# Attention and mixture of experts on one core: the cost table and the ranks of an instruction planner are replaced

## The chip, the core and the metric

The kernel runs on one core of a Trainium2 chip. TensorE (PE in the profile), VectorE (DVE), ScalarE (ACT), GpSimd (POOL) and SyncE (SP) each take their instructions in the order of the program; between engines semaphores keep the order. DMA transfers are issued from SP (loads and stores of the attention part) and from POOL (expert weights, gathers and scatters by index). The metric is the device time of one execution in microseconds (us), lower is better; it is given as the median of several runs.

## The reference

```python
scores = scale * np.matmul(q, k.transpose(0, 1, 3, 2))          # 2 batches, 8 heads, 576 tokens, 64
x = (np.log1p(np.abs(rel)) / psi_i)[..., None]                  # rel: distance of two positions
bias = np.maximum(x @ w1 + b1, 0.0) @ w2                        # 1 -> 32 -> 8 heads, for each pair
attn = softmax(scores + bias)
x = np.matmul(attn, v), heads joined                            # 1152 tokens of 512
logits = x @ w_gate                                             # 8 experts
expert_idx, gate_w = argmax(logits), softmax(logits) at it
# an expert takes at most capacity = 288 tokens, in the order of the tokens
out[token] = gate_w * (relu(x @ w1[e]) @ w2[e])                 # 512 -> 1024 -> 512; 0 if not taken
```

## The kernel before, in words

**Attention.** The work is cut into 40 units: two batches, five row tiles of 128 tokens (the last of 64), four head pairs. A unit n has scores on TensorE (`S`, L195 or L203), a minimum with the bias added on VectorE (`L`, L212), the exponential on ScalarE (`X`, L219), transposes on TensorE (`R` and `T`, L227 to L266), their copies out of PSUM (`C`, L250 and L273) and the product with V (`V`, L289 to L295).

**Bias.** The bias depends on the two positions alone. It is computed once in 36 blocks: hidden rows on three engines (`H`, L122 to L126), a matmul (`M`, L141), an eviction (`E`, L154 or L156) and a store to a scratch tensor in DRAM (`D`, L162, tensor `bd`). Row tiles of it are read back with a skew (`B`, L175 or L178, tile `bt`) as soon as the stores that they need are done. The first scores that can be finished are those of the short row tile t = 4, whose bias comes from the first four blocks.

**Experts.** When a row tile is done, its gate logits are made (`BL`, `BT`, `BC`) and its rows are turned, scaled and stored to DRAM (`BM`, `BX`, `BD`, tensor `xd`). After groups of row tiles the tokens are counted for each expert (`GA`, `GB`, `GK`; the count in PSUM is compared at L451 to L457) and the experts with most tokens are chosen (`P`). For the chosen expert z = 0, 1 (and z = 2 for one small block of tokens) the places of its tokens are matched (`MT`, `FE`), copied to a tile `slots` (`FC`, L475, on ScalarE or VectorE), turned by a small matmul (`FT`, L480), made into indices (`FD`, L486 to L489) and used to gather the rows from `xd` (`FG`, L493, POOL, tile `xe`). The expert's weights come in eight pieces of 512 KB (`WL`, L686, POOL, tile `raw`), which are split into a high and a low part (`WH`, L668 or L670; `WO`, L673, tile `wl`), since each product is made of three matmuls. `XM` turns the gathered rows, `FM` is the first layer (L723, twelve matmuls), `FH` and `FL` split its result (`hh`, `hl`, L726 and L730), `Y` the second layer (L764, groups of six matmuls), `YC` and `OT` turn it back, `OY` scales it (L742 or L744), `OS` scatters it to the output (L748, POOL). z = 2 has steps of its own: `xs`, `xsh`, `xsl` (L803 to L809), `SQ`, `ST`, `SH`, `SL`, `Z` (L828). `RC` (L580) and `RL` then count what is left, for experts beyond these three.

**What sets the order.** All of this is written as 1,126 tasks: `task(name, engines, us, fn, after, rank, takes, late, kb)`. `place_tasks` plays them against a clock: of the tasks whose predecessors are placed and whose buffers come free, those that could begin within 0.3 us of the earliest are compared by rank, and the lowest is issued on its engine. The order found so is the order of the program on each engine; the times are used for nothing else. A rank is a number in the code plus an entry of the table `shift` by kind of task. A DMA task has `kb`: the planner keeps one time `moved` for all transfers and lets each land when the one before it has landed, or a fixed time after its issue, plus its `kb` at 390 per us. `late` is a further time until the result counts as there.

The engines start with the same instructions in both kernels (the constants and the first loads); what follows the planned part (experts beyond the first three) is behind a branch.

Of the kernel before, what the change touches and what calls it, by code (L numbers as in the profile page):

```python
# [18 lines left out]
B, H, S, D = 2, 8, 576, 64  # L19
# [9 lines left out]
def kernel(ctx: ExitStack, tc: tile.TileContext, cap, ins, out):  # L29
# [858 lines left out]
    def rest_begin():  # L888
# [3 lines left out]
        for k in range(8):  # L892
# [9 lines left out]
    tasks = {}  # L902


    shift = {('C', True): 4.5, ('E', False): 1.5, ('E', True): 1.5, ('FL', 0): -0.5, ('FM', 0): 4, ('GA', 0): 0.5,
# [8 lines left out]

    def kind(name):
        if not isinstance(name, tuple):
# [29 lines left out]
    def then(*name):  # L946

        return ("then", name)

    TURN = 0.5  # L950

    def place_tasks(start):
        free_at = dict(start)
        array = None
        ends, begun, held, left, moved = {}, {}, {}, dict(tasks), 0.0
        while left:
            best = []
            for name, (engines, us, fn, after, rank, takes, late, kb) in left.items():
                if any((a[1] if a[0] == "then" else a) not in ends for a in after):
                    continue  # L960
                own = engines if len(engines) == 1 and engines != "s" else None
                ready = max([begun[a[1]] if a[0] == "then" else ends[a] if begun[a, "on"] != own else begun[a] for a in after], default=0.0)
                chosen = []
                for pools, users in takes:

                    at = []
                    for pool in pools:
                        seen = held.get(pool, [])
                        k = len(seen) + chosen.count(pool) - bufs[pool]
                        if k < 0:  # L970
                            at.append((0.0, pool))
                        elif k < len(seen) and all(u in ends for u in seen[k]):
                            at.append((max(ends[u] for u in seen[k]), pool))
                    if not at:
                        break
                    t, pool = at[0] if at[0][0] <= ready else min(at)
                    ready = max(ready, t)
                    chosen.append(pool)
                if len(chosen) == len(takes):
                    e = min(engines, key=lambda e: (max(free_at[e], ready) + us[e], e))  # L980
                    turn = e == "e" and array not in (None, shape(name)[0])
                    best.append((max(free_at[e], ready), rank + TURN * turn, name, e, chosen))
            first = min(b[0] for b in best)
            at, rank, name, e, chosen = min((b for b in best if b[0] <= first + 0.3), key=lambda b: (b[1], b[0]))
            engines, us, fn, after, rank, takes, late, kb = left.pop(name)
            for pool, (pools, users) in zip(chosen, takes):
                held.setdefault(pool, []).append(users)
            took = us[e]
            if e == "e":
                took += 0.096 * (array not in (None, shape(name)[0]))  # L990
                array = shape(name)[1]
            free_at[e] = at + took
            ends[name] = at + took + after_us[e] + late
            begun[name], begun[name, "on"] = at + took, None if late else e
            if kb:
                moved = max(moved, at + took + 0.7) + kb / 390.0
                ends[name] = moved
            fn(*([e] if len(engines) > 1 else []), *(p for p, (pools, _) in zip(chosen, takes) if len(pools) > 1))

    def chain(name, engines, us, gen, after=(), rank=0.0, takes=()):  # L1000
# [10 lines left out]
    for n, blk in enumerate(blocks):  # L1011
        m = span(blk)
        rank = -8.0 + n if n < 4 else 4 * ((n - 4) // 8) - 1.0 + 0.4 * ((n - 4) % 8)
        for c in range(4):
            engines = "p" if c == 3 and n >= 4 else "dap" if c == 2 and n >= 4 or c == 3 else "da"
            task(("H", n, c), engines, {"d": 0.12 + m * 1.1e-3, "a": 0.2 + m * 0.83e-3, "p": m * 3.4e-3},
                 (lambda e="p", n=n, c=c: hidden(n, c, e)), 
                 after=[("H", n - 3, k) for k in range(4)] if n >= 3 else [], rank=rank - 1.2, takes=[("hid", [("M", n)])])
        task(("M", n), "e", 0.06 + m * 1.67e-3 + 0.06 * (m > 512), (lambda w=None, n=n: bias_mm(n, w or bias_psum(n)[0])), after=[("H", n, c) for c in range(4)], rank=rank,
             takes=[(bias_psum(n), [("E", n)])])  # L1020
        task(("E", n), "da", {"d": 1.0, "a": 0.98}, (lambda e, n=n: bias_out(n, e)), after=[("M", n)], rank=rank + 0.1,
             takes=[("bo", [("D", n)])])
        task(("D", n), "s", 0.45, (lambda n=n: bias_store(n)), after=[("E", n)], rank=rank, kb=340)

    for i, (b, t) in enumerate(order):
        n0 = unit0[b, t]
        if i:
            task(("Q", b, t), "s", 0.45, (lambda b=b, t=t: dma_q(b, t)), after=[slot(n0 - 8), then("B", 0, 4, 1)], rank=n0 - 5.0,
                 takes=[("q", [("S", n0 + 3)])], kb=256)
        if (b, t) == (1, 0):  # L1030
            continue
        for g in range(4 if t < 4 else 2):
            users = [("L", n0 + g, z) for z in range(2)] if t < 4 else [("L", n0 + 2 * g + z, 0) for z in range(2)]
            if (b, t) == (0, 0):
# [1 line left out]
            k = order.index((0, t))  # L1036
            dep = [("D", n) for n in (range(4) if t == 4 else range(8 * k - 4, 8 * k + 4))]
            task(("B", b, t, g), "s", 0.45 if t < 4 else 1.2, (lambda b=b, t=t, g=g: dma_bias(b, t, g)), after=dep + [slot(n0 - 6)],
                 rank=n0 - 2.0 + g, takes=[("bt", users)], kb=690)
    for hp in range(4):  # L1040
        task(("K", 1, hp), "s", 0.45, (lambda hp=hp: dma_k(1, hp)), after=[slot(8 + 2 * hp)], rank=17.0, kb=288)
        for b in range(2):
            users = [("V", unit0[b, t] + hp) for t in range(NT)]
            task(("VL", b, hp), "s", 0.45, (lambda b=b, hp=hp: dma_v(b, hp)), after=[slot(17) if b else slot(hp - 1) or then("B", 0, 4, 1)],
                 rank=20.0 * b + hp - 1, takes=[("v", users)], kb=320)
    task("wg", "s", 0.45, lambda: nc.sync.dma_start(out=wgt, in_=ins["wg"]), after=[slot(1)], rank=4.0, kb=32)
    task("route", "s", 2.7, route_const, after=[slot(6)], rank=12.0, kb=300)

# [28 lines left out]
    for i, (b, t) in enumerate(order):  # L1077
# [7 lines left out]
        task(("BC", b, t), "d", 0.8, (lambda b=b, t=t: tile_c(b, t)), after=[("BT", b, t)], rank=n + 1.3)  # L1085
        task(("BM", b, t), "e", 0.48, (lambda w="pt", b=b, t=t: tile_b(b, t, w)), after=[("BL", b, t)], rank=n + 1.2, takes=[(spare, [("BX", b, t)])])
        task(("BX", b, t), "d", 0.64, (lambda b=b, t=t: tile_x(b, t)), after=[("BM", b, t), ("BC", b, t)], rank=n + 1.5, takes=[("x", [("BD", b, t)])])
        task(("BD", b, t), "s", 0.45, (lambda b=b, t=t: tile_d(b, t)), after=[("BX", b, t)] + ([then("FG", 1, 2), then("FG", 2, 0)] if i > 7 else []), rank=n + 1.3, kb=256)
    for g in range(3):
        n = (22.0, 34.0, 44.0)[g]  # L1090
        chain(("GA", g), "d", [0.5, 0.7, 0.3], group_a(g), after=[("BC", b, t) for b, t in groups[g]] + ["route"]
# [17 lines left out]
    for z in range(3):  # L1109
# [7 lines left out]
        for a in range(na):  # L1117
            task(("FG", z, a), "p", 1.25, (lambda z=z, nt=nt, a=a: fetch_rows(z, X[z // 2], nt, a)),
                 after=[("FD", z), ("pools", "clear", "late")[z]] + [("BD", *bt) for g in range(2 if z else 1) for bt in groups[g]],
                 rank=r, late=4.2 if z < 2 else 3.0)  # L1120
    task("pools", "p", 1.4, ffn_pools, after=[("D", n) for n in range(36)] + [slot(18)], rank=20.0)
    task("late", "p", 0.6, late_pools, after=[("V", n) for n in range(NU - 4, NU)] + ["pools"], rank=40.0)
    for a in range(3):
        task(("O", a), "s", 0.45, (lambda a=a: fill_out(a)), after=["pools", slot(33 + a)], rank=34.0, kb=768)
    task("clear", "p", 1.4, lambda: nc.gpsimd.memset(X[0], 0.0), after=[("XM", 0, k) for k in range(4)], rank=33.0)

    for z in range(3):
        for c in range(8):
# [5 lines left out]
            else:  # L1134
# [3 lines left out]
                wait = [] if z == 1 else [("Y", 0, 3, 3)] if c < NW else [("FM", 1, 2 * (c - NW) + 1)]  # L1138
            raw = (lambda c=c, nraw=nraw: RAW[c % nraw])
            task(("WL", z, c), "p", 1.0, (lambda z=z, c=c: weights_load(z, c)), after=dep + [("P", z), then("WL", z, c - 1) if c else then("WL", z - 1, 7) if z else None],  # L1140
                 rank=r, takes=takes, kb=524)
            task(("WH", z, c), "ad", {"a": 0.97, "d": 0.66}, (lambda e, z=z, c=c, raw=raw: split_hi(e, wbuf(z, c)[0], raw())),
                 after=[("WL", z, c)] + wait + (["late"] if z == 1 else []), rank=r + 2)
            task(("WO", z, c), "d", 1.14,
# [205 lines left out]
```

## Time and profile before

| | us |
|---|---|
| median of 3 runs | 278.26 |
| lowest, highest | 274.85, 279.24 |
| the profiled execution's own time | 276.28 |
| its span, first to last instruction | 274.6 |
| TensorE busy | 243.3 (89% of the span) |
| VectorE, ScalarE, GpSimd busy | 194.6, 180.2, 107.3 |
| mean granted TensorE clock | 0.974 of full |

The profile is of one execution, whose own time lies 1.7 us above its span. A share of the whole span hides stages: the stretches and the single waits have to be read one by one. "Granted clock" is the share of TensorE's 2.4 GHz that it was given; 0.5 is 1.2 GHz.

### The profile page before, as it was taken

Reading aid. Unit: us, or ns where it says so; the run is one execution under the profiler, and the core shown is the slowest. Engines: PE = TensorE matmul, PEld = TensorE weight load, DVE = VectorE, ACT = ScalarE, POOL = GpSimd, SP = SyncE. Lnnn points to the kernel's source line nnn. Section 1 sums busy time; section 2 is a strip of 40 time slices with the busy share of each in tenths; the row PEclk is TensorE's granted clock in tenths of the full one; section 3 lists DMA queues with packets and bytes.
Section 4 is the critical chain, followed back from the end, with each engine's and each line's share of the span. In section 5 each row is a group of like instructions: output and inputs, shape, how many; then the busy total and the mean of one; then the engine's idle time right before and its main releaser. Section 6 shows DMA issues by size and latency. Waiting matters only on the chain.

```text
span 274.6 us, 7405 instructions
## 1 busy us (share of the span) xinstructions
PE 243.3 (89%) x2820; PEld 188.2 (69%) x2820; DVE 194.6 (71%) x544; ACT 180.2 (66%) x412; POOL 107.3 (39%) x112
## 2 busy tenths in 40 slices
PE   1995989989999999999969999989989699989950
PEld 0631546557655788888757788878879699979930
DVE  3984989979578666588867975858857779786100
ACT  4897798979899876778857987745232366241400
POOL 2999899999570200000115130120055154500130
PEclk9999999999999999999997999999999979999995
DMA  6589999799698751797698999030145981820030
GB/s 161 206 272 288 373 299 361 230 337 349 188 361 325 250 193 42 219 355 236 175 357 240 347 290 371 17 117 2 41 135 189 375 335 41 264 92 2 2 98 7
DMA packets 26619, 58.63 MB, mean 213 GB/s; under 512 B 3572, under 2 KB 4340, under 8 KB 26576
## 3 DMA queue, kind: packets, MB, share of 16 engines
q1 hardware_dynamic: 22224, 43.02, 47.1%
q0 software_dynamic: 4352, 15.06, 16.4%
q8 instruction: 24, 0.39, 0.6%
q14 instruction: 19, 0.16, 0.2%
HBM read 41.36 MB, written 16.99 MB: 212 GB/s over the span
## 4 chain that ended last, share of the span: by engine, by line
PE 43%; issue 10%; DMA 8%; DVE 6%; POOL 4%; ACT 3%; POOLq 1%; DVEq 0%; ACTq 0%
PE s L195 10%; PE av L289 9%; DMA raw<-in_w_dram 5%; PE tt L227 4%; PE pt L723 3%; DMA xe<-xd,sli 3%; PE s L764 2%; POOL out_dram L748 2%; PE tt L141 2%; PE pt L344 2%; PE tt L764 1%; DVE ed L212 1%; ACT wh L668 1%; PE s L203 1%; PE pt L141 1%
## 5 line engine op out<-in xcount | busy, mean ns | idle before, releaser
L122 POOL TENSOR_SCALAR hid<-c_u,nbv 128x400 f32<-128x400 f32 (+17 forms) x48 | 68.7, 1446 | 6.3 <-PE tt L141 4.2
L212 DVE CUSTOM_DVE_ANT_0 ed<-s,bt 128x576 f32<-128x576 f32 x72 | 51.9, 755 | 22.9 <-PE s L227 10.8
L219 ACT ACTIVATE ed<-ed,mn 128x576 f32<-128x576 f32 x72 | 56.0, 785 | 5.8 <-DVE mn L212 5.7
L250 ACT COPY at<-tt 128x512 f32<-128x512 f32 x71 | 39.0, 590 | 17.7 <-PE tt L227 16.1
L195 PE MATMUL s<-kraw,q 64*128 64x288 f32 x256 | 42.2, 436 | 1.8 <-DVE rt L273 1.6
L289 PE MATMUL av<-at,vt 128*64 128x128 f32 x512 | 35.0, 278 | 0.0
L686 POOL DMA_DIRECT2D raw<-in_w_dram x24 | 13.4, 562 | 49.8 <-DVE wl L673 32.3
L195 PEld LDWEIGHTS s<-kraw,q 64*128 64x128 f32 x256 | 24.8, 190 | 11.7 <-issue 4.4
L289 PEld LDWEIGHTS av<-at,vt 128*64 128x64 f32 x512 | 27.5, 136 | 5.3 <-issue 3.8
L124 ACT ACTIVATE hid<-c_u,c_v 128x528 f32<-128x528 f32 (+17 forms) x44 | 28.2, 680 | 2.9 <-DVE c_v L528 2.9
L126 DVE TENSOR_SCALAR hid<-c_u,c_v 128x432 f32<-128x432 f32 (+17 forms) x52 | 29.6, 617 | 0.1
L673 DVE TENSOR_TENSOR wl<-raw,wh 128x1024 fp32r<-128x1024 f32 x24 | 28.6, 1218 | 0.0
L227 PE MATMUL tt<-c_ident,ed 64*128 64x64 f32 x512 | 22.8, 226 | 0.1
L227 PEld LDWEIGHTS tt<-c_ident,ed 64*128 64x128 f32 x512 | 20.0, 141 | 2.9 <-issue 0.4
L668 ACT CAST wh<-raw 128x1024 fp32r<-128x1024 f32 x13 | 13.6, 1046 | 11.3 <-DMA raw<-in_w_dram 8.0
L434 POOL TENSOR_SCALAR tokv<-s 128x5 bf16<-128x5 f32 (+2 forms) x3 | 0.6, 206 | 51.7 <-DVE s L428 51.7
L141 PE MATMUL pt<-hid,c_w2bd 128*32 128x336 f32 (+12 forms) x152 | 18.0, 511 | 2.7 <-ACT bo L156 1.5
L748 POOL DMA_INDIRECT out_dram<-y,sli x7 | 8.5, 1211 | 27.6 <-ACT sh L842 19.3
L141 PE MATMUL tt<-hid,c_w2bd 128*32 128x512 f32 (+11 forms) x152 | 15.6, 474 | 0.2 <-ACT at L250 0.2
L670 DVE CAST wh<-raw 128x1024 fp32r<-128x1024 f32 x11 | 7.6, 695 | 10.5 <-DMA raw<-in_w_dram 9.3
L219 ACT ACTIVATION_READ_ACCUMULATOR ed<-ed,mn 128x1 f32 x72 | 14.7, 204 | 0.0
L156 ACT ACTIVATE bo<-pt,corr,c_rv 128x192 f32<-128x192 f32 (+23 forms) x24 | 13.0, 596 | 2.1 <-PE pt L141 1.9
(266 smaller groups left out, 518.0 us busy)
## 6 DMA issues: line engine op xcount, KB each, us to landing
bt<-bd SPq DMA_DIRECT2D x28, 576.0 KB, 6.1
raw<-in_w_dram POOLq DMA_DIRECT2D x24, 512.0 KB, 5.8
bd<-bo SPq DMA_DIRECT2D x36, 295.5 KB, 5.3
vt<-in_v_dram SPq DMA_DIRECT2D x8, 320.0 KB, 5.5
kraw<-in_k_dram SPq DMA_DIRECT2D x8, 288.0 KB, 4.7
bt<-bd SPq DMA_DIRECT2D x8, 288.0 KB, 7.3
out_dram<-y SPq DMA_DIRECT2D x3, 768.0 KB, 10.8
q<-in_q_dram SPq DMA_DIRECT2D x8, 256.0 KB, 6.4
```

The lines of the kernel that those rows point to most:

```text
L122: nc.gpsimd.tensor_scalar(hid[:, :m], wu[:, :m], nbv[:, w:w + 1], None, op0=ALU.max)
L124: nc.scalar.activation(hid[:, :m], wu[:, :m], AF.Relu, bias=bvw[:, w:w + 1])
L126: nc.vector.tensor_scalar(hid[:, :m], wu[:, :m], bvw[:, w:w + 1], 0.0, op0=ALU.add, op1=ALU.max)
L141: nc.tensor.matmul(ps[32 * c:32 * c + 32, lo:hi], lhsT=w2bd, rhs=hids[n, c][:, lo:hi], start=True, stop=True, tile_position=(0, 32 * c))
L195: nc.tensor.matmul(ps[i][:, r, :HALF], lhsT=q[p, hp], rhs=k[p, r * HALF:(r + 1) * HALF], start=True, stop=True, tile_position=(64 * i, 0))
L212: nc.vector.tensor_tensor_reduce(out=ed.rearrange("p (r j) -> p r j", r=2), in0=ps[:, :, :HALF], in1=bias.rearrange("p (r j) -> p r j", r= ...
L219: nc.scalar.activation(ed, ed, AF.Exp, scale=-1.0, bias=mns.pop((n, i)), accum_out=total)
L227: nc.tensor.transpose(out[r][:w], ed[p, o:o + w], ident[p, p], tile_position=(64 * r, 0))
L250: nc.scalar.copy(o, v)
L289: nc.tensor.matmul(av[p, hp], lhsT=vt[:, j, i], rhs=at[:, 4 * i + j] if j < 4 else rt, start=(j == 0), stop=(j == 4), tile_position=(0, r))
L668: nc.scalar.copy(hi, raw)
L673: (nc.vector if eng == "d" else nc.gpsimd).tensor_tensor(lo, raw, hi.bitcast(F32), op=ALU.subtract)
```

## The change

Two tables of numbers and four rules of the planner are replaced; no task is added, removed or changed in what it computes. (1) `shift`, the corrections to the ranks, is a new table. (2) A transfer lands `kb`/390 after the later of its issue plus 1.2 us (0.7 before) and the landing before it, and its users are then placed 0.9 us (0 before) plus `late` behind that; the `kb` of nearly all transfers are new. (3) Gathers (`FG`) now have a `kb` and stand in the same row of transfers; before they had a fixed 4.2 or 3.0 us. (4) A successor that may run on one of several engines waits for a `late` result too; a comparison of names let it off before. (5) TensorE's tasks count double before 9.0 us.

```diff
-    shift = {('C', True): 4.5, ('E', False): 1.5, ('E', True): 1.5, ('FL', 0): -0.5, ('FM', 0): 4, ('GA', 0): 0.5,
...
+    shift = {('C', True): 1, ('E', False): -1, ('E', True): 5.5, ('FE', 1): 2, ('FE', 2): 1, ('FH', 0): -2,
...
     TURN = 0.5
+    COLD = 9.0
...
             if e == "e":
+                took *= 2 if at < COLD else 1
                 took += 0.096 * (array not in (None, shape(name)[0]))
...
-            begun[name], begun[name, "on"] = at + took, None if late else e
+            begun[name], begun[name, "on"] = at + took, "late" if late else e
             if kb:
-                moved = max(moved, at + took + 0.7) + kb / 390.0
-                ends[name] = moved
+                moved = max(moved, at + took + 1.2) + kb / 390.0
+                ends[name] = moved + 0.9 + late
...
-        task(("D", n), "s", 0.45, (lambda n=n: bias_store(n)), after=[("E", n)], rank=rank, kb=340)
+        task(("D", n), "s", 0.45, (lambda n=n: bias_store(n)), after=[("E", n)], rank=rank, kb=363)
...
-                 rank=n0 - 2.0 + g, takes=[("bt", users)], kb=690)
+                 rank=n0 - 2.0 + g, takes=[("bt", users)], kb=718)
...
-                 rank=r, late=4.2 if z < 2 else 3.0)
+                 rank=r, kb=470 if z < 2 else 160)
...
-                 rank=r, takes=takes, kb=524)
+                 rank=r, takes=takes, kb=568, late=0.8)
```

**What it does to the order, first place: SP at the start.** SP's queue from the stores of the first four bias blocks (tensor `bd_68`) to the first load of that bias (`bt`, two halves of 288 KB a load). Before:

```order
L162 DMA bd_68<-bo 128x591 x4
L105 DMA vt<-in_v_dram 128x640
L162 DMA bd_67<-bo 128x591 x2
L1046 DMA wgt<-in_wg_dram 128x128
L105 DMA vt<-in_v_dram 128x640
L178 DMA bt<-bd_68 64x2x576 x2
L162 DMA bd_67<-bo 128x591 x2
L178 DMA bt<-bd_68 64x2x576 x2
```

Now:

```order
L162 DMA bd_68<-bo 128x591 x4
L162 DMA bd_67<-bo 128x591 x2
L105 DMA vt<-in_v_dram 128x640
L178 DMA bt<-bd_68 64x2x576 x4
L105 DMA vt<-in_v_dram 128x640
L100 DMA q<-in_q_dram 128x512
L162 DMA bd_67<-bo 128x591 x2
```

The gate weights and one V load (64 and 320 KB) moved behind the bias load, and its second pair of halves no longer waits for two stores. On TensorE one more bias block (`M` of n = 11) now stands ahead of the third scores.

**Second place: ScalarE at two copies of `slots`.** ScalarE where the first expert's slots are copied (L475, the row with 288 columns). Before:

```order
L250 COPY at<-tt 128x2x4x64 x2
L219 ACTIVATE ed,sums<-ed,mn 128x576 x2
L668 CAST wh_1734<-raw_1741 128x1024
L475 CAST slots<-pt 128x288
L250 COPY at<-tt 128x2x4x64 x2
```

Now:

```order
L250 COPY at<-tt 128x2x4x64 x2
L219 ACTIVATE ed,sums<-ed,mn 128x576 x2
L250 COPY at<-tt 128x2x4x64
L475 CAST slots<-pt 128x288
L250 COPY at<-tt 128x2x4x64
```

The split of a weight piece (`wh` from `raw`) that stood ahead of the copy is gone from ScalarE; it stands on VectorE, behind the index step that the copy leads to. The third expert's slots (96 columns), on ScalarE, before:

```order
L668 CAST wh_3350<-raw_1742 128x1024
L767 COPY yt<-pt 128x288
L668 CAST wh_3354<-raw_3365 128x1024
L475 CAST slots<-pt 128x96
L668 CAST wh_3358<-raw_3367 128x1024
```

Now:

```order
L332 COPY lT<-s 128x128
L726 ACTIVATE hh<-pt 128x288
L475 CAST slots<-pt 128x288
L726 ACTIVATE hh<-pt 128x288 x2
L475 CAST slots<-pt 128x96
L315 COPY xT<-av 128x4x64
```

The second expert's slots (288 columns) were copied by VectorE before. Both copies now stand among results of the first layer, and all splits of the second expert's weights on ScalarE come later.

**Third place: the last count on VectorE.** VectorE where the third group of tokens is counted (L451, the first of ten small operations up to L457, on which `RC` on TensorE waits). Before:

```order
L673 TENSOR_TENSOR wl_3349<-raw_1741,wh_3348 128x1024
L673 TENSOR_TENSOR wl_3351<-raw_1742,wh_3350 128x1024
L670 CAST wh_3356<-raw_3366 128x1024
...
L673 TENSOR_TENSOR wl_3353<-raw_3364,wh_3352 128x1024
L451 TENSOR_TENSOR m<-pt,rows 128x8
```

Now:

```order
L673 TENSOR_TENSOR wl_1741<-raw_3464,wh_1740 128x1024
L673 TENSOR_TENSOR wl_3447<-raw_3465,wh_3446 128x1024
L673 TENSOR_TENSOR wl_3449<-raw_3466,wh_3448 128x1024
L809 TENSOR_TENSOR xl<-av,xh 128x4x96
L673 TENSOR_TENSOR wl_3451<-raw_3467,wh_3450 128x1024
L673 TENSOR_TENSOR wl_3453<-raw_3468,wh_3452 128x1024
L451 TENSOR_TENSOR m<-pt,rows 128x8
```

Before, the count stood behind the fourth of the second expert's eight pieces, and twelve `wl` steps came after it; now it stands behind the last piece of the third expert. On TensorE `RC` moved with it, from behind the second of the second expert's eight `FM` to behind `SQ` of q = 0.

## Rows read from the trace of the kernel before

**Rows 1.** Windows: a stretch, its length, each engine's busy time (instructions), granted clock, DMA share, GB/s

```profile
20.00:30.00 10.00, 6.79 (x42) 2.31 (x39) 6.20 (x14) 6.68 (x15) 10.00 (x10) 1.00 1.01 316
...
140.00:150.00 10.00, 7.73 (x96) 6.09 (x94) 6.74 (x18) 5.53 (x13) 3.45 (x4) 0.83 0.93 313
...
210.00:220.00 10.00, 7.76 (x67) 7.28 (x65) 6.66 (x14) 4.38 (x10) 3.82 (x8) 0.97 0.97 364
220.00:230.00 10.00, 10.00 (x72) 9.77 (x72) 7.85 (x37) 7.48 (x12) 4.20 (x8) 0.86 0.57 218
...
260.00:270.00 10.00, 4.92 (x22) 3.13 (x20) 0.00 (x0) 0.83 (x2) 3.09 (x4) 0.86 0.26 73
270.00:274.60 4.60, 0.00 (x0) 0.00 (x0) 0.00 (x0) 0.00 (x0) 0.00 (x0) 0.50 0.00 0
sum 274.60, PE 243.26 PEld 188.17 DVE 194.60 ACT 180.17 POOL 107.27; mean PE 8.69 PEld 6.72 DVE 6.95 ACT 6.43 POOL 3.83
```

**Rows 2.** TensorE's waits: what waited for what: us in total, times, longest

```profile
PE pt L480 <- ACT slots L475: 4.5, 2, 2.3
PE s L203 <- DVE mn L212: 3.1, 1, 3.1
...
PE pt L764 <- DVE hl L730: 1.1, 1, 1.1
PE s L828 <- ACT xh L806: 1.0, 1, 1.0
PE pt L141 <- DVE bo L154: 1.0, 1, 1.0
```

**Rows 3.** The first bias load: SP's timeline, the load's landing, VectorE's first use

```profile
17.27 0.45 SPq L1046 DMA_DIRECT2D wgt<-in_wg_dram  x1
...
18.55 2.30 SPq L178 DMA_DIRECT2D bt<-bd  x2
...
bt<-bd SPq DMA_DIRECT2D x2, 288.0 KB, 5.9
...
25.30 0.76 DVE L212 CUSTOM_DVE_ANT_0 ed<-s,bt 128x576 f32<-128x576 f32 x1 [3.81 <-DMA bt<-bd]
```

**Rows 4.** ScalarE's timeline at the first expert's slots

```profile
143.00 1.04 ACT L668 CAST wh<-raw 128x1024 fp32r<-128x1024 f32 x1 [3.31 <-issue]
143.95 0.39 ACT L475 CAST slots<-pt 128x288 bf16<-128x288 f32 x1
```

**Rows 5.** ScalarE's timeline at the third expert's slots

```profile
217.70 1.04 ACT L668 CAST wh<-raw 128x1024 fp32r<-128x1024 f32 x1 [2.56 <-DMA raw<-in_w_dram]
```

**Rows 6.** Chain in order of time: first layer, second layer, third expert, transposes

```profile
195.80 1.79 PE pt L723 x12
...
249.89 0.80 PE s L764 x6
...
253.28 1.42 PE av L828 x12
...
257.89 0.45 PE pt L777 x4
```

**Rows 7.** Landing of a row store and of two gathers (queue free, queue loaded)

```profile
xd<-x SPq DMA_DIRECT2D x1, 256.0 KB, 2.0
...
xe<-xd,sli POOLq DMA_INDIRECT x1, 3.4
...
xe<-xd,sli POOLq DMA_INDIRECT x1, 8.1
```

**Rows 8.** Timelines of VectorE and POOL late: a count's first step, result splits, last splits, last load

```profile
222.04 0.17 DVE L451 TENSOR_TENSOR m<-pt,rows 128x8 f32<-128x8 f32 x1 [0.49 <-PE pt L419]
...
230.36 0.45 DVE L730 SCALAR_TENSOR_TENSOR hl<-s,hh 128x288 fp32r<-128x288 f32 x1
...
247.70 3.48 DVE L673 TENSOR_TENSOR wl<-raw,wh 128x1024 fp32r<-128x1024 f32 x3
...
239.53 0.54 POOL L686 DMA_DIRECT2D raw<-in_w_dram  x1 [2.82 <-DVE wl L673]
```

More of the change, by code (lines that the diff above doesn't have):

```diff
@@ L1028 @@
             task(("Q", b, t), "s", 0.45, (lambda b=b, t=t: dma_q(b, t)), after=[slot(n0 - 8), then("B", 0, 4, 1)], rank=n0 - 5.0,
-                 takes=[("q", [("S", n0 + 3)])], kb=256)
+                 takes=[("q", [("S", n0 + 3)])], kb=195)
         if (b, t) == (1, 0):
@@ L1038 @@
             task(("B", b, t, g), "s", 0.45 if t < 4 else 1.2, (lambda b=b, t=t, g=g: dma_bias(b, t, g)), after=dep + [slot(n0 - 6)],
-                 rank=n0 - 2.0 + g, takes=[("bt", users)], kb=690)
+                 rank=n0 - 2.0 + g, takes=[("bt", users)], kb=718)
     for hp in range(4):
-        task(("K", 1, hp), "s", 0.45, (lambda hp=hp: dma_k(1, hp)), after=[slot(8 + 2 * hp)], rank=17.0, kb=288)
+        task(("K", 1, hp), "s", 0.45, (lambda hp=hp: dma_k(1, hp)), after=[slot(8 + 2 * hp)], rank=17.0, kb=222)
         for b in range(2):
@@ L1044 @@
             task(("VL", b, hp), "s", 0.45, (lambda b=b, hp=hp: dma_v(b, hp)), after=[slot(17) if b else slot(hp - 1) or then("B", 0, 4, 1)],
-                 rank=20.0 * b + hp - 1, takes=[("v", users)], kb=320)
+                 rank=20.0 * b + hp - 1, takes=[("v", users)], kb=273)
     task("wg", "s", 0.45, lambda: nc.sync.dma_start(out=wgt, in_=ins["wg"]), after=[slot(1)], rank=4.0, kb=32)
@@ L1087 @@
         task(("BX", b, t), "d", 0.64, (lambda b=b, t=t: tile_x(b, t)), after=[("BM", b, t), ("BC", b, t)], rank=n + 1.5, takes=[("x", [("BD", b, t)])])
-        task(("BD", b, t), "s", 0.45, (lambda b=b, t=t: tile_d(b, t)), after=[("BX", b, t)] + ([then("FG", 1, 2), then("FG", 2, 0)] if i > 7 else []), rank=n + 1.3, kb=256)
+        task(("BD", b, t), "s", 0.45, (lambda b=b, t=t: tile_d(b, t)), after=[("BX", b, t)] + ([then("FG", 1, 2), then("FG", 2, 0)] if i > 7 else []), rank=n + 1.3, kb=195)
     for g in range(3):
@@ L1123 @@
     for a in range(3):
-        task(("O", a), "s", 0.45, (lambda a=a: fill_out(a)), after=["pools", slot(33 + a)], rank=34.0, kb=768)
+        task(("O", a), "s", 0.45, (lambda a=a: fill_out(a)), after=["pools", slot(33 + a)], rank=34.0, kb=606)
     task("clear", "p", 1.4, lambda: nc.gpsimd.memset(X[0], 0.0), after=[("XM", 0, k) for k in range(4)], rank=33.0)
```

14 rows, old and new, of the table shift are left out of this document.

## The prediction

> **What bounds the kernel now.** I read the windows first, then TensorE's waits, then the timelines of the engines named there. TensorE is busy 243.3 of 274.6 us, VectorE 194.6, ScalarE 180.2 [rows 1]: no other engine comes near it, so the end is set by TensorE's work, which the change leaves alone, and by what TensorE waits for. It is idle for 274.6 - 243.3 = 31.3 us. The last two windows show 5.1 + 4.6 = 9.7 us of that at the end (the last product is done, the last rows are scaled and scattered) [rows 1], which a new order of the same tasks can't shorten. Of the rest, some 5.6 us lie before there is anything to multiply. About 16 us are left in the middle, and [rows 2] name most of them: 4.5 us in two waits of nearly equal length for the copy of `slots` on ScalarE, 3.1 in one wait of the scores for VectorE's minimum, then many of 0.2 to 1.1.
>
> The two long waits cost more than their length. In the three windows around them the granted clock is 0.83, 0.97 and 0.86 [rows 1]; with only the levels 1 and 0.5 that is (0.17 + 0.03 + 0.14) x 10 = 3.4 us lost to the half clock. It was full in the window of the 3.1 us wait [rows 1], so I count no such loss there.
>
> Why ScalarE is late is in [rows 4] and [rows 5]. Both times the copy (0.39 us the first) stands right behind a weight split of 1.04 us before which ScalarE sat idle for 3.31 and 2.56 us; the second idle time is put down to the landing of `raw`, the first to nothing that the profile shows, but that split reads `raw` too. The order put a consumer of a transfer ahead of the landing, and all that follows on that engine stood behind it. The wait of 3.1 us has the same root: VectorE's first minimum begins at 25.30, 3.81 us late, on the landing of `bt` [rows 3].
>
> **The change part by part.** All sums are made against the profiled execution, 276.28 us, of which 1.7 lie outside the span.
>
> *(a) First bias load.* The load was issued at 18.55, behind the gate weights (issued at 17.27) and a V load, and its halves landed 5.9 us after their issue; VectorE's first use follows at 25.30 [rows 3]. Gate weights and V load now come later: the issue is 18.55 - 17.27 = 1.3 us earlier, and 384 KB less stand ahead, 1.2 us at the 316 GB/s of that window, whose DMA engines were busy throughout [rows 1]. So it lands 2.5 us earlier, and the 3.1 us of [rows 2] shrink to 0.6. An `M` has moved into that place too, so TensorE has work there if its hidden rows are ready. What is late next is GpSimd's share of the hidden rows and the queue of stores behind which the next bias tile waits; they can take the whole gain back. Bounds 0 and -3.1; I take -2.5, by the rows of the load itself.
>
> *(b) The two copies of `slots`.* At the first, ScalarE has nothing ahead of the copy but a copy of a transposed tile that TensorE has long finished; the `wh` split now runs on VectorE behind the index step, so a late piece of weights holds no slot. At the third expert's copy ScalarE has only results of the first layer ahead, and the second expert's splits all stand later. Between the match and the use of `slots` TensorE has one attention product (first) and one short one (third), each longer than the 0.39 us copy. So -4.5 us of waits [rows 2] and, if no wait as long comes elsewhere, -3.4 us of half clock: -7.9. Bounds 0 and -7.9; I take -7.5, leaving 0.4 for a late copy.
>
> *(c) Shorter waits.* Three lose their cause. The second layer waited 1.1 for `hl` of the last first-layer step; seven of its groups on other buffers now come ahead of that place, before it were three. `SQ` waited 1.0 for `xh`, which ScalarE made behind two weight splits; `xs` now stands eight tasks before `SQ` and not four, and `xsh` behind splits whose pieces were asked for earlier. One `M` waited 1.0 for an eviction [rows 2] that VectorE made behind a minimum without its bias; the eviction at that place is now ScalarE's. That is -3.1. But such waits come with any order that leaves tenths of a microsecond between producer and user. Bounds 0 and -3.1; I take half, -1.6.
>
> *(d) What the new order risks.* Two places have little in reserve (below, first and second rival). I charge 0.5 for both.
>
> Sum: -2.5 - 7.5 - 1.6 + 0.5 = -11.1, so 265.2 for the profiled execution. The median of before stands 2.0 above its profiled execution; I do not know where the other will lie, and take 1.3 of these 2.0: **266.5 us**, 4.2% under the median of before. All bounds together (-3.1 - 7.9 - 3.1 = -14.1) give 262.2.
>
> **The rivals.** *First, slower: the last count holds TensorE.* `RC` on TensorE waits for ten small operations on VectorE (0.17 each, 1.7 us [rows 8]) that now stand behind the last `wl` of the third expert; before, it came before twelve of them. From the first `FM` of the second expert to `RC` TensorE has 8 `FM`, 10 `Y`, one `SQ` and some transposes: with matmuls 0.80/6 = 0.133 apart [rows 6] that is 8 x 1.6 + 10 x 0.8 + 1.4 + 2.3 = 24.5 us. VectorE has 14 `wl` at 3.48/3 = 1.16, 8 `hl` at about 0.45, two evictions and an `xl` at about 0.6 each, and the count [rows 8]: 16.2 + 3.6 + 1.8 + 1.7 = 23.3, and must first wait some 0.5 for the turned result. The reserve is 0.7 us. In the trace VectorE finished the last `wl` at 247.70 + 3.48 = 251.2, since POOL issued the last piece only at 239.53, after waiting for a buffer [rows 8]. After `RC`, TensorE still has 6 `Y`, 3 `SQ`, 4 `Z` and seven groups of transposes: 4.8 + 4.3 + 5.7 + 2.5 = 17.3 us [rows 6]. If the splits end no earlier than now, then 251.2 + 1.7 + 0.3 + 17.3 + 9.7 (the end) + 1.7 (half clock, after a wait that long) + 1.7 (outside the span) = 283.6 us, slower than before. It turns slower than the median once the last `wl` ends after 283.6 - 278.3 = 5.3 us earlier than 251.2, that is 245.9; my forecast has it near 234. For it: by this sum VectorE has next to no idle time in that stretch. Against: the pieces were late because buffers came free late, and in the new order the second expert's splits run without the count between them.
>
> *Second: the gather behind a late store.* The turning of row tile 2 of batch 1 (`BM`) has moved from before the fourth `FM` to after the first part of the second layer; the second expert's gather needs its stored rows. The chain from there to `XM` is `BX` (0.7), store (2.0 to landing), three gathers 1.3 apart with a clearing of 0.6 between, the last landing after 3.4 [rows 7]: 0.7 + 2.0 + 2.6 + 0.6 + 3.4 + about 1 for waits = 10.3 us. TensorE's work in between: one `FM` and nine `Y` (1.8 + 7.2 [rows 6]) and an estimated 2.4 of short steps, 11.4. With a loaded queue a gather landed after 8.1 instead of 3.4 [rows 7]; then `XM` waits 4.7 - 1.1 = 3.6 us, and another 1.7 for the half clock: 266.5 + 5.3 = 271.8, or 273 if the store is late as well. The Trainium skill (DMA: Bandwidth & Descriptors, section "Anatomy of one DMA — SWDGE (gpsimd) path") fits a transfer from GpSimd as 2.0 us plus its bytes at 436 GB/s; for 96 rows of 2 KB that is an estimated 2.5 us, the reserve would be 2.0 us and this rival nearly out. The rows have 3.4 at best and 8.1 at worst, so the sum keeps to them.
>
> *Third: the front is held elsewhere.* Every hidden row on GpSimd and every store stays; if they, not the order, set the pace of the first 60 us, (a) comes back in full and (c) does not come: 266.5 + 2.5 + 1.6 = 270.6.
>
> *Fourth: no change.* The consumers still meet late landings because these shift with the order, and the waits come back under other names, half clock included: about 277.
>
> **How the numbers follow.** Forecast 62%; first rival (slower) 8%; second 13%; third 11%; fourth 6%. The range, 262 to 273, takes the forecast with its bounds, the third rival and the second; the first and fourth (14%) are left out. 2% of 278.26 is 5.6 us, about what runs that spread from 274.85 to 279.24 can tell from no change; faster by more means under 272.7. Forecast, third rival and a fifth of the second: 0.76. Within 2%: the rest of the second and the fourth, 0.16. Slower: 0.08.
>
> **What the next profile must show.** (b) is right if `FT` (L480) no longer stands among TensorE's longer waits and the windows from 130 to 230 have a granted clock of 1.00; wrong if a wait of about 2 us stands under another name and a window shows 0.8 to 0.9. (a) is right if VectorE's first minimum begins near 22.5 to 23 and the scores' wait there is under 1 us; if it begins there but the ninth unit is no earlier than before, the third rival holds. (c) shows in the sum of waits of 0.3 to 1.2 us. The first rival shows as a wait of L580 for VectorE, the second as a wait of L703 (or its copies) for `xe`, each with the half clock behind it. The forecast fails most likely where landings were fitted in a queue that the new order fills differently: at the gather and at the last weights.

## The result and the profile after

| | before | after |
|---|---|---|
| median of 6 runs each, us | 277.36 | 262.76 |
| lowest, highest | 274.85, 279.24 | 260.85, 265.88 |
| ratio, 95% interval | | 0.948 (0.940 to 0.956) |
| the profiled execution's own time | 276.28 | 260.9 |
| its span | 274.6 | 259.1 |
| TensorE busy, mean granted clock | 243.3, 0.974 | 238.8, 0.989 |

The kernel is 14.6 us faster; the forecast was 11.8 below the median it was made against, 266.5 in a range of 262 to 273, so the measured median lies in the range, at its lower end. The ratios, here and below, are made from the runs within 1.5% of the fastest of their kernel, so they can differ from the ratio of the medians. The windows of the kernel after that answer to [rows 1]:

```profile
20.00:30.00 10.00, 8.41 (x82) 3.51 (x74) 8.89 (x21) 8.98 (x21) 10.00 (x10) 1.00 1.00 296
...
140.00:150.00 10.00, 10.00 (x146) 7.99 (x143) 9.53 (x25) 8.09 (x21) 3.51 (x4) 1.00 0.99 323
...
210.00:220.00 10.00, 10.00 (x80) 9.98 (x79) 9.84 (x14) 8.85 (x14) 7.65 (x9) 1.00 1.03 409
220.00:230.00 10.00, 10.00 (x78) 10.00 (x77) 9.64 (x12) 7.76 (x12) 0.00 (x0) 1.00 0.53 209
...
sum 259.10, PE 238.84 PEld 185.97 DVE 193.99 ACT 180.94 POOL 106.94; mean PE 9.19 PEld 7.15 DVE 7.46 ACT 6.96 POOL 4.11
```

The granted clock is 1.00 in all of them, and TensorE is busy throughout from 200 to 240 us. VectorE and ScalarE have as much to do as before; they stand still less while TensorE does. Its waits after, for [rows 2] (what waited for what: us in total, times, longest), in full:

```profile
PE pt L534 <- DMA c_w2bd<-in_w2bd_dram: 4.7, 1, 4.7
PE pt L141 <- ACT bo L156: 1.0, 2, 0.6
PE s L141 <- ACT hid L124: 0.9, 1, 0.9
PE pt L141 <- ACT at L250: 0.9, 1, 0.9
PE s L195 <- DVE rt L273: 0.8, 2, 0.4
PE tt L241 <- DVE bo L154: 0.8, 2, 0.5
PE s L203 <- DVE mn L212: 0.8, 1, 0.8
PE pt L703 <- DVE xl L711: 0.6, 1, 0.6
```

L480 is gone, L764 and L828 too, and after the start nothing is longer than 0.9. The two copies of `slots` on ScalarE's timeline, for [rows 4] and [rows 5], and VectorE's first minimum, for [rows 3]:

```profile
137.28 0.41 ACT L475 CAST slots<-pt 128x288 bf16<-128x288 f32 x1
...
197.44 0.24 ACT L475 CAST slots<-pt 128x96 bf16<-128x96 f32 x1 [1.46 <-PE pt L471]
...
23.64 0.76 DVE L212 CUSTOM_DVE_ANT_0 ed<-s,bt 128x576 f32<-128x576 f32 x1 [1.04 <-DMA bt<-bd]
```

Both copies begin as soon as TensorE has made the match. The first bias load on SP's timeline, and its landing (KB each, median us from issue):

```profile
16.70 2.77 SPq L178 DMA_DIRECT2D bt<-bd  x2
...
bt<-bd SPq DMA_DIRECT2D x2, 288.0 KB, 5.8
```

The span fell by 15.5 us: TensorE's idle time before its last product went from 21.7 to 10.7 (-11.0), its busy time from 243.3 to 238.8 (-4.4, of which the two half-clock stretches are 3.4), the end from 9.7 to 9.6.

### The profile page after: what moved, and what is told of

The parts are those of the page before. It is cut to its first block, busy times and chain, and to the rows that moved or that the text cites. A ratio compares the mean times of both kernels' runs of the same rounds, so it can differ in the third digit from the quotient of the medians.

```text
span 259.1 us, 7407 instructions
## 1 busy us (share of the span) xinstructions
PE 238.8 (92%) x2820; PEld 186.0 (72%) x2820; DVE 194.0 (75%) x551; ACT 180.9 (70%) x405; POOL 106.9 (41%) x112
## 4 chain that ended last, share of the span: by engine, by line
PE 69%; DMA 11%; issue 6%; DVE 5%; ACT 3%; POOL 2%; POOLq 0%; SPq 0%; DVEq 0%
PE s L195 11%; PE av L289 11%; PE tt L227 5%; PE s L764 5%; PE pt L723 5%; DMA bd<-bo 5%; PE tt L141 3%; PE pt L141 3%; DMA raw<-in_w_dram 3%; PE tt L764 3%; PE pt L764 3%; DMA bt<-bd 2%; PE s L203 2%; PE s L141 2%; PE tt L723 2%
## 5 line engine op out<-in xcount | busy, mean ns | idle before, releaser
L122 POOL TENSOR_SCALAR hid<-c_u,nbv 128x384 f32<-128x384 f32 (+17 forms) x48 | 68.7, 1447 | 2.2 <-PE tt L141 1.3
L250 ACT COPY at<-tt 128x512 f32<-128x512 f32 x68 | 37.6, 590 | 17.9 <-PE tt L227 14.0
L195 PE MATMUL s<-kraw,q 64*128 64x288 f32 x256 | 40.8, 426 | 0.9 <-DVE rt L273 0.8
L126 DVE TENSOR_SCALAR hid<-c_u,c_v 128x464 f32<-128x464 f32 (+17 forms) x52 | 29.2, 609 | 0.1
L124 ACT ACTIVATE hid<-c_u,c_v 128x448 f32<-128x448 f32 (+16 forms) x44 | 26.9, 668 | 2.9 <-DVE c_v L528 2.9
L141 PE MATMUL pt<-hid,c_w2bd 128*32 128x496 f32 (+11 forms) x144 | 17.4, 513 | 1.8 <-ACT bo L156 1.0
L141 PE MATMUL tt<-hid,c_w2bd 128*32 128x512 f32 (+11 forms) x160 | 18.0, 471 | 0.1
L668 ACT CAST wh<-raw 128x1024 fp32r<-128x1024 f32 x16 | 16.8, 1049 | 0.5 <-DMA raw<-in_w_dram 0.4
L156 ACT ACTIVATE bo<-pt,corr,c_rv 128x192 f32<-128x192 f32 (+25 forms) x26 | 14.1, 595 | 0.9 <-PE pt L141 0.6
L493 POOL DMA_INDIRECT xe<-xd,sli x7 | 8.7, 1248 | 14.5 <-DVE hl L730 8.2
```

The lines of the kernel that those rows point to most:

```text
L122: nc.gpsimd.tensor_scalar(hid[:, :m], wu[:, :m], nbv[:, w:w + 1], None, op0=ALU.max)
L124: nc.scalar.activation(hid[:, :m], wu[:, :m], AF.Relu, bias=bvw[:, w:w + 1])
L126: nc.vector.tensor_scalar(hid[:, :m], wu[:, :m], bvw[:, w:w + 1], 0.0, op0=ALU.add, op1=ALU.max)
L141: nc.tensor.matmul(ps[32 * c:32 * c + 32, lo:hi], lhsT=w2bd, rhs=hids[n, c][:, lo:hi], start=True, stop=True, tile_position=(0, 32 * c))
L195: nc.tensor.matmul(ps[i][:, r, :HALF], lhsT=q[p, hp], rhs=k[p, r * HALF:(r + 1) * HALF], start=True, stop=True, tile_position=(64 * i, 0))
L250: nc.scalar.copy(o, v)
```

## The experiments

For a move by hand the planner's order is kept as a list, single tasks are shifted in it (and given an engine), and the list is then issued; nothing else moves. Rules and tables are changed in the planner itself. Medians of 4 to 11 runs:

| run | kernel | median, us | ratio to before run beside it (95%) |
|---|---|---|---|
| e1 | before, first copy of `slots` freed | 275.84 | 1.005 (1.002 to 1.008) |
| e2 | before, both copies freed | 276.19 | 1.000 (0.988 to 1.013) |
| e3 | before, first bias load earlier | 276.26 | 0.996 (0.989 to 1.003) |
| e4 | before, e2 and e3 | 276.22 | 0.994 (0.986 to 1.001) |
| e7 | e4, and the next late thing at both places | 277.26 | none: its runs lay from 272.68 to 280.23 |
| e5 | new rules, old table | 265.44 | 0.963 (0.951 to 0.974) |
| e6 | new table, old rules | 280.40 | 1.015 (1.004 to 1.025) |
| e9 | before, weights' landing 2.2 later, with rule (4) | 268.32 | 0.966 (0.953 to 0.979) |
| e10 | e5 without rule (4) | 294.05 | 1.057 (1.045 to 1.068) |
| e8 | after, one split put back | 266.35 | 0.962 (0.951 to 0.972) |
| e11 | after, SP's old start | 264.53 | 0.957 (0.950 to 0.964) |
| e12 | after, 3.5 us more ahead of the last count | 268.24 | 0.970 (0.963 to 0.978) |

Before was run beside them three times, with medians of 275.48 (e1 to e4), 278.0 (e5 to e8) and 276.73 (e9 to e12). The profiled executions of e1, e4, e10 and e11 lie 0.9 to 3.4 us above their medians; they are read for the waits, not for the time.

### The causes of the long waits, taken away by hand

e1, in the kernel before (e2 adds the last line):

```diff
+    MOVES = [
+        (("WH", 0, 0), "d", ("C", 27, 2), "behind"),
+        (("WH", 0, 1), "d", ("FD", 0), "behind"),
+        (("WH", 1, 4), "a", ("FC", 2), "behind"),
+    ]
```

> The kernel before, with nothing moved but two weight splits: the first expert's splits 0 and 1 go behind the second minimum and behind the index step, so that the first copy of slots has no split ahead of it on ScalarE. Theory (step b of the prediction: the split ahead of the copy makes the wait, the wait makes the half clock): the 2.3 us wait of L480 and the half clock behind it (1.7 us) go, 277.4 - 4.0 = 273.4, and the windows 140:150 show a granted clock of 1.00. Rival (the gain of the new order is made of many small fits, and a single late copy only hides other late work): the wait comes back at the next user of ScalarE or VectorE, over 276.

> As the run before, and the second expert's split 4 moved behind the third copy of slots. Theory (step b): both waits of L480 (2.27 and 2.24 us) and both half-clock stretches (1.7 us each) go, 277.4 - 7.9 = 269.5; more than half of the whole gain of 14.6 us from four moved instructions. Rival (many small fits): over 275.

e3:

```diff
+    MOVES = [
+        (("B", 0, 4, 1), "s", ("B", 0, 4, 0), "behind"),
+        (("VL", 0, 2), "s", ("D", 8), "behind"),
+        ("wg", "s", ("D", 10), "behind"),
+    ]
```

> The kernel before, with nothing moved but SP's queue at the start: the second pair of bias halves directly behind the first, the gate weights and one V load behind later stores. Theory (step a): the first bias load lands some 2 us earlier, the 3.1 us wait of the scores shrinks to about 1, and 1 to 2.3 us stay at the end: 275.1 to 276.4. Rival (third rival of the prediction: the front is paced by the hidden rows and the stores): the wait shrinks but the ninth unit is no earlier, 277.4 within 0.5.

> The kernel before with both moves of slots and the SP queue of the run before: the three causes of the long waits taken away by hand. Theory (steps a and b add): 277.4 - 7.9 - 1.5 = 268; what the new order has beyond that (262.8) is then 5 us of short waits (step c, sized at 1.6 in the prediction). Rival (they hide each other): less than the sum of the parts, over 271.

None of the four gained anything that can be told from noise: the ratios lie between +0.5% and -0.6% (e2's interval is the widest, -1.2% to +1.3%), the medians 0.1 to 0.3% above that of before. e3's median lies in the range of its theory only because that was reckoned from 277.4; before ran at 275.5 beside it. The moves did what they say: L480 has no wait in e1's first place nor in either place of e2, and the wait of the scores is 2.5 in e3 and 1.4 in e4 instead of 3.1. The time went into other waits. From the first expert's match to its first layer TensorE has the same instructions in the same order in before and in e1 to e4; first before, then e1:

```profile
140.47 0.42 PE L471 MATMUL pt<-match,tokv 128*32 128x288 bf16 x5
...
164.68 0.40 PE L723 MATMUL pt<-xh,wh 128*128 128x288 f32 x1
```

```profile
143.50 0.42 PE L471 MATMUL pt<-match,tokv 128*32 128x288 bf16 x5
...
168.57 0.40 PE L723 MATMUL pt<-xh,wh 128*128 128x288 f32 x1
```

That is 24.2 and 25.1 us, and 22.5 in e2 and 24.5 in e4. The clock was at half for 3.4 us in that stretch in all but e2; without the 1.7 us that this costs they are 22.5, 23.4, 22.5 and 22.8. So the 2.3 us of the copy's wait did not come out at the other end. Part of TensorE's waits in e1:

```profile
PE s L195 <- DVE rt L273: 2.8, 3, 2.1
PE s L203 <- DVE mn L212: 2.8, 1, 2.8
PE pt L480 <- ACT slots L475: 2.2, 1, 2.2
PE pt L703 <- DMA xe<-xd,sli: 2.2, 2, 1.6
```

The last row is new: it takes the place of the first copy's 2.3. (The 2.1 in the first row is no work of the move: it lies at 97.8 us, ahead of all that e1 changed, and VectorE waited there for a bias tile; this wait was 0.4 in before and between 0.5 and 1.9 in e2, e3, e4 and e7.) VectorE's minimum there, in e1:

```profile
96.10 0.76 DVE L212 CUSTOM_DVE_ANT_0 ed<-s,bt 128x576 f32<-128x576 f32 x1 [3.87 <-DMA bt<-bd]
```

POOL's timeline shows why the gathers are late, first before, then e1:

```profile
145.47 0.54 POOL L686 DMA_DIRECT2D raw<-in_w_dram  x1 [6.83 <-DVE slt L487]
146.48 1.05 POOL L493 DMA_INDIRECT xe<-xd,sli  x1 [0.48 <-issue]
147.84 1.01 POOL L493 DMA_INDIRECT xe<-xd,sli  x1 [0.30 <-issue]
149.15 0.96 POOL L493 DMA_INDIRECT xe<-xd,sli  x1 [0.30 <-issue]
```

```profile
146.96 0.96 POOL L686 DMA_DIRECT2D raw<-in_w_dram  x1 [5.28 <-DVE slt L487]
148.22 1.05 POOL L493 DMA_INDIRECT xe<-xd,sli  x1 [0.30 <-issue]
149.58 2.79 POOL L493 DMA_INDIRECT xe<-xd,sli  x1 [0.30 <-issue]
152.67 0.97 POOL L493 DMA_INDIRECT xe<-xd,sli  x1 [0.30 <-issue]
```

Both times the gathers stand behind the fourth weight piece, which gets its buffer only when VectorE has made a `wl`; VectorE makes that, and then the indices, behind a split. In before this split waited 2.5 us for its piece; in e1 it stands behind two minima and waits for nothing more, but the indices still stand behind it and the `wl`:

```profile
141.73 0.69 DVE L670 CAST wh<-raw 128x1024 fp32r<-128x1024 f32 x1 [2.45 <-DMA raw<-in_w_dram]
```

```profile
144.72 0.68 DVE L670 CAST wh<-raw 128x1024 fp32r<-128x1024 f32 x1
```

From the match (140.47 before, 143.50 in e1) to the first gather it took 6.0 us before and 4.7 in e1, though the copy's wait of 2.3 was gone, and one gather then took 2.8 instead of 1.0 to issue. TensorE came to `XM` sooner after the match and waited there, 0.6 and 1.6 us. In the changed kernel the same stretch is 2.8 us (match at 136.64):

```profile
139.46 1.31 POOL L493 DMA_INDIRECT xe<-xd,sli  x1 [4.93 <-DVE slt L489]
```

In e2 the third expert's copy gave its 2.2 us to L415, which waited 1.9 for VectorE's index step behind another split. e7 asks whether one more step ends the chain; it adds to the moves of e4:

```diff
+        (("FG", 0, 0), "p", ("WL", 0, 3), "ahead"),
+        (("FG", 0, 1), "p", ("WL", 0, 3), "ahead"),
+        (("FG", 0, 2), "p", ("WL", 0, 3), "ahead"),
+        (("WH", 1, 5), "d", ("FD", 2), "behind"),
```

> The run with the three moves by hand, and what was late next there: the first expert's three gathers ahead of the fourth weight piece on POOL, and the second expert's split 5 behind the third expert's index step on VectorE. Theory C (one chain: the removed wait of the copy was followed at once by the next late thing of the same chain, and with that gone too the time falls): the waits of L703 for xe and of L415 for slt (1.8 each, with 1.7 of half clock behind each) go, 269. Rival (the moves by hand only shift waits; every later consumer in the old order also stands ahead of its landing): 274 or more.

The rival holds. The wait of L703 is gone; since the gathers now go first, the pieces behind them land later, and a split on ScalarE that had not been moved holds the next unit's copies. ScalarE and TensorE in e7:

```profile
153.97 1.04 ACT L668 CAST wh<-raw 128x1024 fp32r<-128x1024 f32 x1 [3.05 <-issue]
154.92 1.06 ACT L250 COPY at<-tt 128x512 f32<-128x512 f32 x2
...
156.15 2.40 PE L195 MATMUL s<-kraw,q 64*128 64x288 f32 x8 [2.46 <-ACT rt L273]
```

That is 2.5 us for 1.8, with a half-clock stretch with it in this execution. At L415 a wait of 1.7 stayed: another split, which waited for its piece, and two `wl` still stood ahead of the index step on VectorE.

### Rules or ranks

e5 is the changed kernel with the old `shift`, e6 the kernel before with the new one. e9 is the kernel before with this edit alone; in e10 rule (4) is taken out of e5.

```diff
-            begun[name], begun[name, "on"] = at + took, None if late else e
+            begun[name], begun[name, "on"] = at + took, "late" if late else e
...
-                ends[name] = moved
+                ends[name] = moved + late
...
-                 rank=r, takes=takes, kb=524)
+                 rank=r, takes=takes, kb=568, late=2.2)
```

> The planner's new rules (landings, late, COLD) with the old table of ranks. In the order that comes out no split stands ahead of either late copy of slots, the first gather is issued ahead of the fourth weight piece, and the third expert's index step stands ahead of the splits on VectorE. Theory A (the gain comes from consumers placed behind the landings, which the rules do): most of it is here, 264 to 268 where before is 275.5. Theory B (it comes from the ranks, which were searched with these rules): 270 or more.

> The new table of ranks with the old rules. A split of the first weight piece stands ahead of the first copy of slots on ScalarE, the third expert's match, copy and index step stand ahead of all late pieces. Theory A (rules): 270 to 276. Theory B (ranks): 266 or less.

> The kernel before with one thing changed in the planner: the landings of the expert weights count 2.2 us later (with the rule that lets a successor on two engines wait for that). Table of ranks, all other transfers and TensorE's first 9 us are as before. In the order that comes out the first copy of slots is free, the first gather stands ahead of the fourth piece, but on VectorE a low part still stands ahead of the third expert's index step. Theory A1 (nearly all late consumers were weight splits): 266 to 270. Rival A2 (bias tiles, first load and gathers matter as much): 272 or more.

> The new rules with the old table, less one: a successor that may run on either of two engines is again let off a late result. Since the weights now carry a late, their first splits are placed as if the piece were there at its issue, and they stand ahead of the copies of transposed tiles and of slots. Theory A (consumers ahead of their landings make the waits): all of the gain is lost, 277 or more, with waits over 1 us from 135 to 150 us. Theory B (the table or the other rules make the gain): within 2 us of the 265.4 of the new rules.

The rules carry most of the gain: 3.7% of the 5.2% come without the new ranks, and the new ranks without the rules are 1.5% slower than before, above both ranges that were given for e6. What the ranks add, 1.5%, is less sure, since the intervals of e5 and of the change overlap. The weights alone, which land 2.2 us later for the planner (with 0.1 more for each piece from `kb`) while no byte is moved otherwise, give 3.4%. What the other rules add to that is not told apart: e5 and e9 lie 0.3% from each other, and rules (3) and (5) and the other `kb` were not run by themselves. The waits of e9:

```profile
PE s L203 <- DVE mn L212: 2.9, 1, 2.9
...
PE pt L580 <- DVE acc L457: 1.3, 1, 1.3
PE pt L703 <- DMA xe<-xd,sli: 1.2, 2, 0.7
```

No wait over 1.4 is left behind the front, and the front is as before, as it should be with the old bias loads. e10 makes the error larger: all splits are placed as if the piece were there when it is asked for. ScalarE in e10 sits 5.67 us in front of one, with two copies for TensorE behind it; TensorE waited 4.2 for them:

```profile
148.00 1.04 ACT L668 CAST wh<-raw 128x1024 fp32r<-128x1024 f32 x1 [5.67 <-issue]
148.95 1.07 ACT L250 COPY at<-tt 128x512 f32<-128x512 f32 x2
```

Its further waits are 3.7 (L471), 3.6 (L764) and 2.6 (L723). Rule (4) by itself, without a `late` on the weights, gives the order of before to the last task, so its worth here is only that it lets the other rules work.

### One thing put back into the changed order

e8, e11 and e12, each in the kernel after:

```diff
+    MOVES = [(("WH", 0, 1), "a", ("FC", 0), "ahead")]
```

```diff
+    MOVES = [(("VL", 0, 2), "s", ("B", 0, 4, 0), "ahead"), ("wg", "s", ("VL", 0, 2), "ahead")]
```

```diff
-  split_lo(e, *wbuf(z, c), raw())
+  [split_lo(e, *wbuf(z, c), raw()) for _ in range(4 if (z, c) == (2, 7) else 1)]
```

> The changed kernel, with one split (the first expert's piece 1) put back ahead of the first copy of slots on ScalarE; its piece lands at 139.0 and TensorE asks for the turned slots at 138.2. Theory (each wait costs its length and the half clock behind it, where the rest of the order has room): a wait of 2.3 to 2.7 at L480, and 1.7 of half clock in perhaps half of the executions, 262.8 + 3.4 = 266.2. Rival (the wait is swallowed by the room that the order has behind it): within 1 of 262.8.

> The changed kernel with SP's old start: the gate weights and one V load again ahead of the first bias load. Step a of the prediction: the wait of the scores grows from 0.8 to 2.5 or 3 us, with 1.7 of half clock behind it in some executions, 264.5 to 267. Third rival (the first 60 us are paced by hidden rows and stores): within 1 us of 262.8.

> The changed kernel with the low part of the third expert's last weight piece computed four times in place of once: 3 x 1.17 = 3.5 us more on VectorE ahead of the last count, nothing else moved. It tests the reserve of the prediction's first rival: the trace has the count done at 231.8 and TensorE asking for it at 232.5, a reserve of 0.7. Theory: a wait of 3.5 - 0.7 = 2.8 us at L580 and 1.7 of half clock in some executions, 265.6 to 267.3. Rival (the wait is hidden, since other engines give it back before the end): within 1 us of 262.8.

e8: 3.6 us over the kernel after, 3.4 were expected; the intervals of the two ratios just overlap (0.951 and 0.956), but the wait is there. ScalarE and TensorE:

```profile
141.59 1.04 ACT L668 CAST wh<-raw 128x1024 fp32r<-128x1024 f32 x1 [1.82 <-DMA raw<-in_w_dram]
142.54 0.39 ACT L475 CAST slots<-pt 128x288 bf16<-128x288 f32 x1
...
142.99 0.30 PE L480 MATMUL pt<-quart,slots 128*96 128x6 bf16 x3 [2.30 <-ACT slots L475]
```

The clock fell to half right behind it (0.83 in the window 140 to 150). One of the two splits that e1 took from this place at no gain costs its whole price where nothing else is late.

e11: 1.8 us over after, with a wait of the scores of 3.46; the intervals of the two ratios overlap, so the time alone doesn't settle it. The wait itself varies between executions of one start: 3.1, 2.8, 3.4, 2.9 and 3.5 with the old one (before, e1, e2, e9, e11), 0.8, 1.6 and 2.1 with the new (after, e8, e12). The means, 3.1 and 1.5, differ by 1.6. The half clock comes on top: behind the wait the clock was at half for 3.4 us in e1 and e9, for 6.8 in e2 and e11, and not at all in before; with the new start for 3.4 us in e8 alone.

e12: 5.5 us over after, more than the 2.8 to 4.5 that were expected. The count and the wait for it, VectorE and TensorE:

```profile
238.28 0.17 DVE L457 TENSOR_TENSOR acc<-acc,m 128x8 bf16<-128x8 bf16 x1
...
238.50 0.19 PE L580 MATMUL pt<-acc,ones 128*128 128x8 bf16 x2 [3.22 <-DVE acc L457]
```

3.2 and 1.7 of half clock (0.83 in the window 240 to 250) are 4.9; the other 0.6 is not explained. Nothing was hidden: a late count moves the end by all of it. The first rival was a real danger, 0.7 us away by the trace of after and 0.3 by this one (3.5 added, 3.2 waited).

## Why the prediction was right, and where it was not

**What bounds the kernel** was read rightly: TensorE's busy time without the half clock hardly moved (-1.0, which I did not take apart), the end not at all, and the gain is idle time and clock.

**(a)**, -2.5: the load was issued at 16.70 instead of 18.55 and landed 5.8 us later, before it was 5.9 [rows 3]; the first minimum began at 23.64, not at 22.5 to 23. The load was issued 1.9 earlier and not 1.3, but I had let the 384 KB that no longer stand ahead shorten the flight by 1.2 as well, and they did not: the minimum came 1.7 earlier and not 2.5. In this execution the wait fell by 2.3, since TensorE also came to it 0.7 later, with more done; but 0.8 came back between 36 and 44 us, in waits for ScalarE and VectorE. I also took no half clock for this wait, because the one profile of before had none; the four other executions with this start have it, and with any of them the load would have been priced 1.7 or 3.4 higher. e11 gives 1.8, with its uncertainty. In the old order alone (e3) it gave nothing that can be measured, so the third rival was half right.

**(b)**, -7.5: the size was right (4.5 and 3.4 went, 7.9), the reason incomplete. The step said that the wait goes because no split stands ahead of the copy. e1, e2 and e7 show that this is not enough: the gather behind a weight piece, the index step and the copies of the next unit behind other splits were late too, and took the wait over. In e9, where the planner itself counts the landing later, no wait at these places is over 0.7; that it has to take all of them at once is what e1 to e7 beside e9 speak for, and is not shown one by one. The 3.4 of half clock is in part luck: e3 keeps both waits, and its profile has a half-clock stretch behind one of them only. My fourth rival, waits that come back under other names, is what the hand-made moves do; I gave it 6% for the whole order, and there it did not happen.

**(c)**, -1.6 in bounds of 0 and -3.1: mis-sized. The idle time before the last product fell by 11.0; without 4.5 and 2.3 that is 4.2 in short waits, net of the 0.8 that came back, and above my bound. I had named three waits as the most that could go, and all three went; beside them before had eight of 0.2 to 0.5 behind the first 60 us, after has one of 0.4 and one of 0.6, and from 160 us on no wait over 0.11 us was left. I let half of the named return "with any order that leaves tenths of a microsecond"; this one leaves such tenths at few places.

**(d)**, +0.5: nothing came. The count was done at 231.64 + 0.17 = 231.8, and TensorE had work until 232.5, a reserve of 0.7 as forecast:

```profile
231.64 0.17 DVE L457 TENSOR_TENSOR acc<-acc,m 128x8 bf16<-128x8 bf16 x1
...
232.54 0.20 PE L580 MATMUL pt<-acc,ones 128*128 128x8 bf16 x2
```

For the second rival the third gather was issued at 200.56 and landed after 3.4, at 204.0, and TensorE took its rows at 204.65: 0.7 in hand where I had 1.1. The transfers had room there (the DMA engines were 31% busy from 196 to 204 us), since the gathers go ahead of four weight pieces on POOL:

```profile
200.56 1.23 POOL L493 DMA_INDIRECT xe<-xd,sli  x1 [0.15 <-issue]
201.79 2.20 POOL L686 DMA_DIRECT2D raw<-in_w_dram  x4
```

The landings of the three gathers of the second expert (196 to 201 us) and of the first (139 to 143 us, when the DMA engines were busy throughout), medians:

```profile
xe<-xd,sli POOLq DMA_INDIRECT x3, 3.4
...
xe<-xd,sli POOLq DMA_INDIRECT x3, 7.0
```

The fit of the Trainium skill that the prediction weighed (DMA: Bandwidth & Descriptors, section "Anatomy of one DMA — SWDGE (gpsimd) path"), an estimated 2.5 us for these rows, is under both, and the reserve was nearer to mine than to its 2.0.

The sum was -11.1 for the profiled execution and measured -15.4; 2.6 of the difference is (c), 1.0 the busy time, 0.9 (b) and (d), less 0.2 for (a). All bounds together had given 262.2, and the profiled execution came in at 260.9.

## What to carry to other kernels

On engines that work in order, a wait read from a profile is a price only if nothing else late stands behind it: ask what is late next and next but one before it is counted as a gain. A planner that believes transfers land too early puts many consumers ahead of their landings at once; correcting the landing (here that of the weights, with the rule that makes their users wait for it, 3.4%) was worth more than moving the consumers that the profile names. The old ranks with the new rules kept 3.7 of the 5.2%, the new ranks with the old rules nothing: put the planner's times right first, then its ranks. One profile is one execution: read what a wait costs from several before it goes into a sum. In an order that fits, one misplaced consumer costs its whole wait; price a reserve by adding work to it, as in e12.

## What the runs showed of the hardware

The half clock does not follow from the length of a wait. In the 14 profiled executions TensorE had 22 waits of 2.0 us or more after the first 8 us; with 15 of them, towards their end or within some 2 us behind it, the granted clock fell to 0.5 for 3.4 us (6.8 with one of 3.4 and one of 3.5, among others), with 7 of them it did not, one of them 3.6 long. Of 22 waits between 1.3 and 2.0, six were followed by it. A stretch of 3.4 us at half clock costs a busy TensorE 1.7 us (a window of 10 us then shows 0.83). So 1.7 us behind a wait is what it often costs, not what it must; it may also be a part of why executions of one kernel lie several microseconds apart, which no run here isolates.
